# Second-layer scales by a logarithm and an exponential on ScalarE instead of powers of two

## The chip, the core and the metric

One Trainium2 chip, one of its cores. The metric is the time of one execution on the device, in microseconds (us); lower is better. The kernel before takes 1286.33 us, the median of three runs (1284.23 to 1288.01). A difference of about 0.3%, some 3.9 us, is what a measurement of this kernel can tell from no change.

The engines are called as the profile calls them: PE (matrix multiply; PEld are its weight loads), DVE (VectorE), ACT (ScalarE), POOL (GpSimd) and SP (SyncE, here only a queue that issues DMA transfers). Each engine runs its own list of instructions strictly in the order in which they were recorded; an instruction that waits for a semaphore holds up everything behind it on that engine.

## What is computed

Eight batches of eight heads, 576 rows, 64 columns per head. The attention keeps only scores within `tau` of the row's maximum; a two-layer network with a rational function between the layers follows.

```python
scores = matmul(q, k.T) / sqrt(64)
scores = where(scores >= max(scores) - tau, scores, -1e9)
attn = exp(scores - max(scores)); attn /= sum(attn) + 1e-9
x = attn @ v                                  # 4608 x 512 after the heads are put side by side
h = x @ w_in                                  # 512 x 2048
P = a[0] + a[1]*h + a[2]*h**2 + a[3]*h**3
Q = 1 + abs(b[0])*abs(h) + abs(b[1])*h**2
out = (P / (Q + 1e-6)) @ w_out                # 2048 x 512
```

## The kernel before, in words

**Attention.** The work is cut into units: one pair of heads and one block of 128 rows (64 for the last, odd block). A unit is: scores on PE (L840 to L851), the negated row maximum on DVE (L857, or L859 for an odd block), a thresholding Prelu and an Exp with row sums on ACT (L872, L876), the reciprocal of the sums (L881 or L883 for the sum's scaling on ACT or DVE, L887 for the reciprocal), the probabilities split into two 16-bit parts (L894 on ACT or DVE through the helper `times`, L898 on DVE), a transpose by DMA from SP (L908), and the product with the values on PE (L969). The first batch transposes on PE instead (L914, L921, L926) and uses L952.

**Network.** A step (`moe_ops`) takes 256 rows of `x` and up to four blocks of 128 hidden columns: first layer on PE (L1092), its result scaled out by ACT (L1101), then about ten element-wise passes on DVE and ACT (L1103 to L1144: `f_A`, `f_r2`, `f_q`, `f_r3`, `f_ln`, `f_inv`, `f_e`, `f_n`, `f_g`, `f_gh`, `f_gl`), then the second layer on PE (L1153) and its evacuation (`f_o`, L1159 or L1164). There are 73 steps.

**Scales.** The second layer is fed with 16-bit pieces, so its left operand is brought into range by a scale per batch. `scale_of` (L1275) makes it for each batch and each set of weight groups: 12 runs in all, ten named `gs_m` and two named `gs_r`. A run is: a bound of the result by four short instructions on POOL (`f_bound`), six short DVE instructions on one to four columns (`f_scales`: minimum, mask to an even power of two, maximum, a root made by integer arithmetic on the exponent, two products), and one logarithm on ACT (`f_ln_r`). `f_inv` (L1123) takes its logarithm, `f_n` (L1133) the product `m2r`, and `f_o` the factor `down`.

**Weights.** Both weight matrices arrive as 64-bit words and are decoded and scaled in 32 pieces during the first part (`decode_ops`, `group_ops`: L528 to L610); loads go out from POOL (L573).

**The order.** Every instruction is recorded as an `op` with a key and estimated durations for the engines that could run it; `Plan.order` places the ops one after another by keys, readiness, buffers and prices per engine, and so decides both the order on each engine and, for some ops (`FLEX` and `can`: for example the 16-bit copy `f_gh`, or L881/L883), which of ACT and DVE runs it. `START`, `EARLY` and `PRICE` weigh an engine's time up to about 70 us, up to `EARLY_END`, and after it; `LEAD`, `SPACING`, `ENDK` and `ENDS` set the keys of the network's steps, `WHEN` and `AHEAD_RANK` those of the weights, `V0` and `V1` those of the value loads. In planned idle time of PE before 400 us the plan puts filler matmuls on the identity matrix (L1383), which compute nothing that is used.

Of the kernel before, what the change touches and what calls it, by code (L numbers as in the profile page):

```python
# [31 lines left out]
ENDK, ENDS = 4.7452, 10.130284218  # L32

WHEN = [(-4.7413, 1.827956817), (5.5534, 0.8332), (13.0267, 0.2709), (15.0744, 0.5122)]

V0, V1 = -4.003497408, -3.629280468

SINGLE = 21

# [23 lines left out]

MASK, EVEN = 0x7F800000, 0x7F000000

BOUND = {"POOL": 1.8}

STEEP = 2.0 ** 100

ALL = 2.0 ** 100  # L70
# [3 lines left out]
UP = 2.0 ** -14  # L74
TPD = 1.3

AHEAD_RANK = 2.703269966

AHEAD = 3

# [48 lines left out]
class Plan:  # L129
# [158 lines left out]
def masked_attention_rational_ffn(  # L288
# [16 lines left out]
    P = 128  # L305
# [748 lines left out]
    def moe_ops(ck, f0, nb, p, begins, ends, soon, gs):  # L1054
# [174 lines left out]
        if ends:  # L1229
            prev = None  # L1230
            obox = {}
            through = f0 + nb == NF
            part = Hold("t", 2)
            for tt in range(2):
                old = sums.get((ck, tt))
                obox[tt] = {}
                if old is None:
                    ho = obox[tt]["hold"] = Hold("u", 1) if through else part
                    o = op("ACT", 0.477, p + 0.2 * nb + 1.8, lambda tt=tt, old=old: f_o(tt, old), [last_g2[tt], prev], [ho] if through or tt == 0 else [], [ah[tt]])
                else:  # L1240
                    ho = old[1]
                    o = op("DVE", 0.663, p + 0.2 * nb + 1.8, lambda tt=tt, old=old: f_o(tt, old), [last_g2[tt], prev, old[2]], (), [ah[tt]])
# [11 lines left out]
    def consts(gs):  # L1254


        if gs not in consts_of:
            n = len(gs)
            tab = const.tile([P, n + 3], F32, name=f"gc_{gs[0]}_{n}")
            m2, wmax, top, dn = tab[:, 0:n], tab[:, n:n + 1], tab[:, n + 1:n + 2], tab[:, n + 2:n + 3]  # L1260

            def f_consts():
                io = so[:, gs[0]:gs[-1] + 1]
                nc.vector.tensor_reduce(wmax, wn[:, gs[0]:gs[-1] + 1], AX.X, ALU.max)
                nc.vector.tensor_reduce(top, io, AX.X, ALU.max)
                nc.vector.tensor_scalar(dn, top, osc, 2.0 ** -13, ALU.mult, ALU.mult)
# [3 lines left out]
                nc.vector.tensor_scalar(m2, m2, -2.0 ** 65, None, ALU.mult)  # L1270
            o = op("DVE", 0.95, w_key(gs[-1], 2 * NC), f_consts, [co_b] + [z[y] for z in (wn_done, so_done) for y in gs])
            consts_of[gs] = o, m2, wmax, dn
        return consts_of[gs]

    def scale_of(ck, gs):  # L1275


        kind, b, _ = ck
        run = kind, b, gs
        if run not in scales_of:  # L1280
            n = len(gs)
            done, m2, wmax, dn = consts(gs)
            tab = const.tile([P, 2 * n + 4], F32, name=f"gs_{kind}{b}_{gs[0]}_{n}")
            m2r, lnr = tab[:, 0:n], tab[:, n:2 * n]
            H, s, R, down = (tab[:, 2 * n + i:2 * n + i + 1] for i in range(4))

            def f_top():
                nc.vector.tensor_reduce(R, isx[:, 4 * b:4 * b + 4], AX.X, ALU.max)

            def f_bound():  # L1290
                x = isx[:, b:b + 1] if kind == "m" else R
                e = engines[plan.eng]
                e.tensor_scalar(H, x, wmax, 1.0, ALU.mult, ALU.mult)
                e.tensor_scalar(s, H, c2, H, ALU.add, ALU.mult)
                e.tensor_scalar(s, s, c1, H, ALU.add, ALU.mult)
                e.tensor_scalar(s, s, c0, ct, ALU.add, ALU.mult)

            def f_scales():
                nc.vector.scalar_tensor_tensor(s, H, c1s, s, ALU.add, ALU.min)
                nc.vector.tensor_single_scalar(s.bitcast(I32), s.bitcast(I32), EVEN, ALU.bitwise_and)  # L1300
                nc.vector.tensor_scalar(s, s, SMALL, None, ALU.max)
                nc.vector.tensor_scalar(R.bitcast(I32), s.bitcast(I32), -0.5, float(197 << 23), ALU.mult, ALU.add)
                nc.vector.tensor_scalar(m2r, m2, R, None, ALU.mult)
                nc.vector.tensor_scalar(down, s, dn, None, ALU.mult)
# [6 lines left out]
            o = [done] + [isx_done[x] for x in bs]  # L1311
# [114 lines left out]
```

## Time and profile before

| | before |
|---|---|
| median of 3 runs | 1286.33 us |
| the profiled execution | 1288.7 us |
| its span on the core | 1286.9 us |
| mean granted PE clock | 0.981 |
| PE busy | 1225.7 us (95%) |
| DVE busy | 1224.1 us (95%) |
| ACT busy | 1114.2 us (87%) |
| POOL busy | 262.4 us (20%) |

The span lies 1.8 us inside the profiled execution's own time, and that execution took 2.4 us more than the median of the three. In the views below a group's row gives the busy time of all its instructions, the mean of one in ns, and behind the second bar the idle time of the engine just ahead of them with what ended it. In a timeline a row's first number is the start, the second the duration, both in us; neighbouring short instructions overlap a little, so the step from one start to the next is what an instruction costs its engine. Matmul ends are modelled.

### The profile page before, as it was taken

The page shows a single profiled execution, that of the slowest core. Times are in us where ns is not written, and L with a number is a line of the kernel's source. Part 1 is how long each engine was busy: PE and PEld are TensorE (multiplying, and loading weights), DVE is VectorE, ACT ScalarE, POOL GpSimd, SP SyncE. Part 2 cuts the span into 40 slices and gives each one's busy share as a digit, 9 for nine tenths or more (in the row PEclk, how much of TensorE's full clock was granted, in tenths as well). Part 3 has the DMA queues.
Part 4 walks back from the last instruction along what each step waited for, and adds up shares of the span by engine and source line. Part 5 has one row for each costly group of instructions (what it writes and reads, how often), then busy time and mean ns, then how long its engine had stood idle before and what let it go on. Part 6 is the DMA issues. An engine that isn't in the chain of part 4 may idle for free.

```text
span 1286.9 us, 25594 instructions
## 1 busy us (share of the span) xinstructions
PE 1225.7 (95%) x9520; PEld 799.3 (62%) x9520; DVE 1224.1 (95%) x1871; ACT 1114.2 (87%) x2183; POOL 262.4 (20%) x528
## 2 busy tenths in 40 slices
PE   7899899999999989899999799999999989999998
PEld 6566676566666656566666466656666655656674
DVE  5798999999999999999999899999999999999897
ACT  5898999899997988899999799999899998986564
POOL 3112010013412242134211241134212331000000
PEclk8899999999999999999999899999999989999999
DMA  9434325468545765577645666576756756643001
GB/s 251 152 116 122 111 65 113 94 131 156 123 110 104 142 130 112 113 139 149 122 101 100 119 137 129 95 148 122 149 88 129 140 95 115 123 94 68 17 1 33
DMA packets 338380, 146.67 MB, mean 114 GB/s; under 512 B 314416, under 2 KB 320720, under 8 KB 338256
## 3 DMA queue, kind: packets, MB, share of 16 engines
q1 hardware_dynamic: 316816, 88.19, 38.4%
q0 software_dynamic: 21120, 56.25, 15.8%
q8 instruction: 75, 1.23, 0.4%
q10 hardware_dynamic: 320, 0.59, 0.2%
q14 instruction: 49, 0.40, 0.1%
HBM read 60.30 MB, written 9.44 MB: 54 GB/s over the span
## 4 chain that ended last, share of the span: by engine, by line
PE 29%; DVE 22%; issue 6%; ACT 5%; POOL 1%; DMA 1%; DVEq 0%; ACTq 0%; POOLq 0%
PE banks L1153 12%; PE banks L1092 11%; DVE e L898 5%; PE banks L969 3%; DVE st L857 3%; PE banks L851 3%; DVE g L1144 2%; DVE t L1126 1%; DVE t L1129 1%; DVE t L1112 1%; DVE t L1115 1%; DVE t L1133 1%; DVE t L1136 1%; ACT e L872 1%; DVE hi L339 1%
## 5 line engine op out<-in xcount | busy, mean ns | idle before, releaser
L1153 PE MATMUL banks<-wo,g 128*128 128x512 f16 x1728 | 401.7, 381 | 8.0 <-DVE g L1144 8.0
L1092 PEld LDWEIGHTS <-wi 128*128 128x128 f16 x3456 | 335.2, 99 | 109.6 <-issue 57.8
L1092 PE MATMUL banks<-x,wi 128*128 128x256 f16 x3072 | 362.3, 275 | 19.3 <-ACT t L1101 16.7
L1153 PEld LDWEIGHTS <-g 128*128 128x128 f16 x1728 | 162.5, 99 | 226.7 <-issue 40.9
L876 ACT ACTIVATE e<-e,cf 128x576 f32<-128x576 f32 x288 | 221.3, 775 | 0.3
L872 ACT ACTIVATE e<-banks,st 128x576 f32<-128x576 f32 x288 | 208.6, 736 | 12.6 <-DVE st L866 9.9
L898 DVE SCALAR_TENSOR_TENSOR e<-e,st,hi 128x576 f16<-128x576 f32 x252 | 203.6, 808 | 4.5 <-ACT hi L337 4.2
L337 ACT ACTIVATE hi<-e,st 128x576 f16<-128x576 f32 x183 | 139.0, 768 | 49.5 <-DVE st L887 38.4
L857 DVE TENSOR_REDUCE st<-banks 128x2 f32<-128x1152 f32 x128 | 171.9, 1343 | 10.4 <-PE banks L851 9.9
L851 PE MATMUL banks<-KK,QQ 64*128 64x512 f32 x512 | 148.5, 658 | 0.0
L969 PEld LDWEIGHTS <-V 128*64 128x64 f16 x2520 | 104.2, 111 | 30.6 <-issue 28.1
L969 PE MATMUL banks<-pT,V 128*64 128x256 f16 (+1 forms) x2520 | 121.7, 250 | 1.5 <-DMA pT<-e 1.5
L1101 ACT ACTIVATE t<-banks,hsc 128x512 f32<-128x512 f32 (+1 forms) x192 | 106.4, 573 | 18.1 <-PE banks L1092 17.7
L1119 ACT ACTIVATE t<-t,co 128x1024 f32<-128x1024 f32 (+1 forms) x73 | 82.6, 1132 | 21.5 <-DVE t L1126 20.4
L1112 DVE SCALAR_TENSOR_TENSOR t<-t,co 128x1024 f32<-128x1024 f32 (+1 forms) x73 | 91.9, 1260 | 0.5 <-ACT t L1101 0.5
L1115 DVE SCALAR_TENSOR_TENSOR t<-t,co 128x1024 f32<-128x1024 f32 (+1 forms) x73 | 91.9, 1259 | 0.0
L680 POOL DMA_DIRECT2D QQ<-in_qT_dram x42 | 22.2, 529 | 341.5 <-PE banks L840 192.6
L1144 DVE TENSOR_TENSOR g<-t,g 128x1024 f16<-128x1024 f32 (+1 forms) x73 | 87.6, 1200 | 0.1
L1126 DVE SCALAR_TENSOR_TENSOR t<-t,co,t 128x1024 f32<-128x1024 f32 (+1 forms) x65 | 81.7, 1257 | 0.0
L1129 DVE SCALAR_TENSOR_TENSOR t<-t,co,t 128x1024 f32<-128x1024 f32 (+1 forms) x62 | 77.9, 1257 | 1.9 <-ACT t L1123 1.9
L1136 DVE SCALAR_TENSOR_TENSOR t<-t,co,t 128x1024 f32<-128x1024 f32 (+1 forms) x63 | 79.2, 1257 | 0.1
L724 POOL DMA_DIRECT2D V<-in_v_dram x24 | 18.8, 785 | 272.0 <-PE banks L969 169.8
(186 smaller groups left out, 1690.7 us busy)
## 6 DMA issues: line engine op xcount, KB each, us to landing
KK<-in_kT_dram POOLq DMA_DIRECT2D x84, 144.0 KB, 3.5
t<-in_w_in_dram POOLq DMA_DIRECT2D x16, 512.0 KB, 5.6
t<-in_w_out_dram POOLq DMA_DIRECT2D x16, 512.0 KB, 5.0
V<-in_v_dram POOLq DMA_DIRECT2D x24, 256.0 KB, 4.4
QQ<-in_qT_dram POOLq DMA_DIRECT2D x42, 144.0 KB, 3.2
out_dram<-u POOLq DMA_DIRECT2D x22, 256.0 KB, 3.4
QQ<-in_qT_dram POOLq DMA_DIRECT2D x42, 128.0 KB, 3.4
KK<-in_kT_dram SPq DMA_DIRECT2D x24, 144.0 KB, 3.2
```

The lines of the kernel that those rows point to most:

```text
L337: nc.scalar.activation(dst, src, AF.Identity, scale=factor)
L851: nc.tensor.matmul(d, QQ[r, t * P:(t + 1) * P], KK[r, REM:S], **one)
L857: nc.vector.tensor_reduce(box["st"][:, 0:2], box["both"], AX.X, ALU.max, negate=True)
L872: nc.scalar.activation(ev(hh), box["s"][hh], AF.Prelu, scale=SCALE, bias=box["st"][:, 2 + hh:3 + hh], alpha=STEEP)
L876: nc.scalar.activation(e, e, AF.Exp, scale=passes, accum_out=box["st"][:, 4 + hh:5 + hh])
L898: nc.vector.scalar_tensor_tensor(box["lo"][:, c], ev(hh), box["st"][:, 6 + hh:7 + hh], box["hi"][:, c], ALU.mult, ALU.subtract)
L969: nc.tensor.matmul(dst, V[:, c * P + head * D:c * P + (head + 1) * D], rhs, start=c == 0 and n == 0, stop=c == NT and n == 2)
L1092: nc.tensor.matmul(d, wi_tile(c, f0 + j, hl), x[:, c, :], start=c == 0 and n == 0, stop=c == NC - 1 and n == 2)
L1101: nc.scalar.activation(box["h3"][:, 2 * k:2 * k + 2, sl], psv[:, :, sl], AF.Identity, scale=hsc[:, b2, (f0 + 2 * k) // NC:(f0 + 2 * k) // ...
L1112: nc.vector.scalar_tensor_tensor(box["r"], box["h"], a2, box["h"], ALU.add, ALU.mult)
L1144: nc.vector.tensor_tensor(box["g", x][:, 1, 0:w], box["r"][:, j0 * CT:j1 * CT], box["g", x][:, 0, 0:w], ALU.subtract)
L1153: nc.tensor.matmul(acc[tt], box["g", x][:, y, o:o + P], wo[:, x, f % NC, z], start=begins and j == n == 0, stop=ends and j == nb - 1 and n ...
```

## The change

The six DVE instructions of `f_scales` become two: the minimum stays (`f_min`), and a reciprocal is added (`f_one`). What lay between is done on ACT, as five short activations (`f_roots`): the logarithm `l` of the bound, its exponential with factor -1/2 (the scale `R`, now any number and not a power of two), `l` halved, the product of the group constants with `R`, and their logarithm plus `l`. The logarithm of the group constants alone (`ln2`) is made once per set of groups. Two more short instructions go to POOL: the square of `R` (`f_square`) and, after the reciprocal on DVE, the factor `down` (`f_down`). `f_inv` now waits for `f_roots` only; `f_o` waits for `f_down` as well (`scaled`). The bound on POOL is no longer an op with a table of engines, but is on POOL as it was.

Beside this the planner's numbers are changed, among them these:

```diff
-LEAD, SPACE0, SPACING = 4.776489494, 2.7365, 2.235134465
+LEAD, SPACE0, SPACING = 5.974676841, 2.7365, 2.235134465
-START = {"ACT": 2.072266916, "DVE": 3.23844158}
+START = {"ACT": 2.072266916, "DVE": 2.724283317}
```

`ENDS` goes from 10.13 to 8.45, `AHEAD_RANK` from 2.70 to 1.91, `PRICE` of DVE from 2.95 to 2.54, `EARLY_END` from 1185.1 to 1164.8, `V1` from -3.63 to -3.35, `ENDK` from 4.75 to 5.49, and the third pair of `WHEN` from 13.03 to 13.58.

```diff
-            def f_scales():
+            def f_min():
                 nc.vector.scalar_tensor_tensor(s, H, c1s, s, ALU.add, ALU.min)
-                nc.vector.tensor_single_scalar(s.bitcast(I32), s.bitcast(I32), EVEN, ALU.bitwise_and)
-                nc.vector.tensor_scalar(s, s, SMALL, None, ALU.max)
-                nc.vector.tensor_scalar(R.bitcast(I32), s.bitcast(I32), -0.5, float(197 << 23), ALU.mult, ALU.add)
-                nc.vector.tensor_scalar(m2r, m2, R, None, ALU.mult)
-                nc.vector.tensor_scalar(down, s, dn, None, ALU.mult)
-
-            def f_ln_r():
-                nc.scalar.activation(lnr, m2r, AF.Ln, scale=-0.5)
+
+            def f_roots():
+                nc.scalar.activation(l, s, AF.Ln, bias=small_)
+                nc.scalar.activation(R, l, AF.Exp, scale=-0.5)
+                nc.scalar.activation(l, l, AF.Identity, scale=-0.5)
+                nc.scalar.activation(m2r, m2, AF.Identity, scale=R)
+                nc.scalar.activation(lnr, ln2, AF.Identity, bias=l)
+
+            def f_square():
+                nc.gpsimd.tensor_tensor(s, R, R, ALU.mult)
+
+            def f_one():
+                nc.vector.reciprocal(s, s)
+
+            def f_down():
+                nc.gpsimd.tensor_scalar(down, s, dn, 1.0, ALU.mult, ALU.mult)
...
-            o = op(BOUND, 0, p, f_bound, o)
-            o = op("DVE", 0.8, p, f_scales, [o])
-            o = op("ACT", 0.25, p, f_ln_r, [o])
+            o = op("POOL", 1.8, p, f_bound, o)
+            o = op("DVE", 0.15, p, f_min, [o])
+            o = o1 = op("ACT", 1.1, p, f_roots, [o])
+            o = op("POOL", 0.4, p, f_square, [o])
+            o = op("DVE", 0.1, p, f_one, [o])
+            o = [o1, op("POOL", 0.4, p, f_down, [o])]
```

The instructions that are left stand in another order, since all of them were placed anew. Three places follow, in the order in which the engine runs its rows; a name with a number is one buffer, and the changed kernel numbers lines and buffers a little differently.

DVE before, in batch 0, between the first maximum over the weight pieces (L449 on `wm`) and the one over the values (L449 on `vm`). L737 reduces the fourth pair's values `V`, which a DMA brings; L331 evacuates a transposed block; L344 decodes a weight piece.

```order
L449 TENSOR_REDUCE sc_86<-wm 128x1
L455 TENSOR_SCALAR u_68<-ident,sc_86 128x128
L331 COPY pT_76<-banks 128x128
L737 TENSOR_REDUCE vm_218<-V_140 128x1
L344 ISA t_97<-t_97,u_70 128x512x2
L887 RECIPROCAL st_80<-st_80 128x2
L449 TENSOR_REDUCE sc_87<-vm_218 128x1
```

DVE in the changed kernel, the rows that end with the same reduction of the fourth pair's values (line 342 here is 344 before, 329 is 331, 337 is 339).

```order
L472 TENSOR_SCALAR sw<-sc_86 128x1
L474 RECIPROCAL sw<-sw 128x1
L914 TENSOR_SCALAR u_70<-ident,st_80 128x128
L337 TENSOR_SCALAR wi<-t_95,sw 128x512 x2
L610 SCALAR_TENSOR_TENSOR wi<-t_95,sw,wi 128x512 x2
L610 SCALAR_TENSOR_TENSOR wi<-t_96,sw,wi 128x512 x2
L329 COPY pT_77<-banks 128x128
L342 ISA t_97<-t_97,u_69 128x512x2
L887 RECIPROCAL st_81<-st_81 128x2
L583 TENSOR_REDUCE wm<-t_97 128x1
L737 TENSOR_REDUCE vm_220<-V_142 128x1
```

The reduction that waits for the fourth pair's values stood two places behind the weights' maximum; now the whole scaling of the first weight group (L465 to L474) and its splitting (L337, L610) go ahead of it, with a score reduction, 21 instructions in all.

DVE in the changed kernel, around one of the twelve scale runs, from the minimum (L1304 there) to the reciprocal (L1317 there); L784 splits the next batch's values, L1129 is a pass of the network. Before, the six instructions of `f_scales` stood together.

```order
L1304 SCALAR_TENSOR_TENSOR gs_m_0_4_161<-gs_m_0_4_161,co 128x1
L784 SCALAR_TENSOR_TENSOR V_141<-V_141,sx,u_68 128x640
L784 SCALAR_TENSOR_TENSOR V_142<-V_142,sx,u_69 128x640
L329 COPY V_141<-u_68 128x640
L329 COPY V_142<-u_69 128x640
L1129 SCALAR_TENSOR_TENSOR t_95<-t_95,co,t_96 128x1024
L1317 RECIPROCAL gs_m_0_4_161<-gs_m_0_4_161 128x1
```

Five other instructions now stand between the two; while they run, ACT's roots and POOL's square have to be done.

More of the change, by code (lines that the diff above doesn't have):

```diff
@@ L28 @@
 B2, B3, BA, B1, BH = [(0, 1, 2), (3, 4, 5)], [(0, 1, 2)], [(3,), (4,), (5,)], [(7,), (6,), (5,)], [(5,), (6,)]
-LEAD, SPACE0, SPACING = 4.776489494, 2.7365, 2.235134465
-ENDK, ENDS = 4.7452, 10.130284218
-WHEN = [(-4.7413, 1.827956817), (5.5534, 0.8332), (13.0267, 0.2709), (15.0744, 0.5122)]
-V0, V1 = -4.003497408, -3.629280468
+LEAD, SPACE0, SPACING = 5.974676841, 2.7365, 2.235134465
+ENDK, ENDS = 5.488906476, 8.452439532
+WHEN = [(-4.7413, 1.827956817), (5.5534, 0.8332), (13.580547557, 0.2709), (15.0744, 0.5122)]
+V0, V1 = -4.003497408, -3.352127285
 SINGLE = 21
@@ L64 @@
 MASK, EVEN = 0x7F800000, 0x7F000000
-BOUND = {"POOL": 1.8}
 STEEP = 2.0 ** 100
@@ L75 @@
 TPD = 1.3
-AHEAD_RANK = 2.703269966
+AHEAD_RANK = 1.912895801
 AHEAD = 3
@@ L88 @@
          "vc": {"ACT": 0.7, "DVE": 0.25}, "twice": {"ACT": 0.2, "DVE": 0.13}}
-START = {"ACT": 2.072266916, "DVE": 3.23844158}
+START = {"ACT": 2.072266916, "DVE": 2.724283317}
 START_END = 70.459703715
 EARLY = {"ACT": 2.0183, "DVE": 2.9268}
-EARLY_END = 1185.086141893
-PRICE = {"ACT": 0.7389, "DVE": 2.949233976}
+EARLY_END = 1164.835153503
+PRICE = {"ACT": 0.7389, "DVE": 2.538788989}
 TOL = {"PE": 0.098890645, "ACT": 0.1137, "DVE": 0.0398, "POOL": 0.1, "DMA": 0, "GD": 0}
@@ L375, in masked_attention_rational_ffn @@
     ones = bass.AP(one.tensor, one.offset, [list(one.ap[0]), [0, P]])
+    small_ = const.tile([P, 1], F32, name="small")
+    nc.vector.memset(small_, SMALL)
     one16 = const.tile([P, 2], BF16, name="one16")
@@ L1204, in moe_ops @@
         ln = op("ACT", act(nb) + 0.09, p + 0.7, f_ln, [q, r3])
+        sd, scaled = sd
         iv = [op("ACT", act(x[2] - x[1]) + 0.09, p + 0.75, lambda x=x: f_inv(*x), [ln, sd]) for x in parts]
@@ L1238, in moe_ops @@
                     ho = obox[tt]["hold"] = Hold("u", 1) if through else part
-                    o = op("ACT", 0.477, p + 0.2 * nb + 1.8, lambda tt=tt, old=old: f_o(tt, old), [last_g2[tt], prev], [ho] if through or tt == 0 else [], [ah[tt]])
+                    o = op("ACT", 0.477, p + 0.2 * nb + 1.8, lambda tt=tt, old=old: f_o(tt, old), [last_g2[tt], prev, scaled], [ho] if through or tt == 0 else [], [ah[tt]])
                 else:
                     ho = old[1]
-                    o = op("DVE", 0.663, p + 0.2 * nb + 1.8, lambda tt=tt, old=old: f_o(tt, old), [last_g2[tt], prev, old[2]], (), [ah[tt]])
+                    o = op("DVE", 0.663, p + 0.2 * nb + 1.8, lambda tt=tt, old=old: f_o(tt, old), [last_g2[tt], prev, scaled, old[2]], (), [ah[tt]])
                 prev = o
@@ L1258, in consts @@
             n = len(gs)
-            tab = const.tile([P, n + 3], F32, name=f"gc_{gs[0]}_{n}")
-            m2, wmax, top, dn = tab[:, 0:n], tab[:, n:n + 1], tab[:, n + 1:n + 2], tab[:, n + 2:n + 3]
+            tab = const.tile([P, 2 * n + 3], F32, name=f"gc_{gs[0]}_{n}")
+            m2, ln2 = tab[:, 0:n], tab[:, n:2 * n]
+            wmax, top, dn = (tab[:, 2 * n + i:2 * n + i + 1] for i in range(3))
             def f_consts():
@@ L1269, in f_consts, with f_ln2 @@
                 nc.vector.tensor_scalar(m2.bitcast(I32), m2.bitcast(I32), 1, MASK, ALU.logical_shift_right, ALU.bitwise_and)
-                nc.vector.tensor_scalar(m2, m2, -2.0 ** 65, None, ALU.mult)
-            o = op("DVE", 0.95, w_key(gs[-1], 2 * NC), f_consts, [co_b] + [z[y] for z in (wn_done, so_done) for y in gs])
-            consts_of[gs] = o, m2, wmax, dn
+                nc.vector.tensor_scalar(m2, m2, -2.0 ** 72, None, ALU.mult)
+            def f_ln2():
+                nc.scalar.activation(ln2, m2, AF.Ln, scale=-0.5)
+            key = w_key(gs[-1], 2 * NC)
+            o = op("DVE", 1.2, key, f_consts, [co_b] + [z[y] for z in (wn_done, so_done) for y in gs])
+            consts_of[gs] = [o, op("ACT", 0.25, key, f_ln2, [o])], m2, ln2, wmax, dn
         return consts_of[gs]
@@ L1281, in scale_of @@
             n = len(gs)
-            done, m2, wmax, dn = consts(gs)
-            tab = const.tile([P, 2 * n + 4], F32, name=f"gs_{kind}{b}_{gs[0]}_{n}")
+            done, m2, ln2, wmax, dn = consts(gs)
+            tab = const.tile([P, 2 * n + 5], F32, name=f"gs_{kind}{b}_{gs[0]}_{n}")
             m2r, lnr = tab[:, 0:n], tab[:, n:2 * n]
-            H, s, R, down = (tab[:, 2 * n + i:2 * n + i + 1] for i in range(4))
+            H, s, R, l, down = (tab[:, 2 * n + i:2 * n + i + 1] for i in range(5))
             def f_top():
@@ L1291, in f_bound @@
                 x = isx[:, b:b + 1] if kind == "m" else R
[L1292 to L1296, printed above, removed]
-            def f_scales():
[L1299 to L1304, printed above, removed]
-            def f_ln_r():
-                nc.scalar.activation(lnr, m2r, AF.Ln, scale=-0.5)
+                nc.gpsimd.tensor_scalar(H, x, wmax, 1.0, ALU.mult, ALU.mult)
+                nc.gpsimd.tensor_scalar(s, H, c2, H, ALU.add, ALU.mult)
+                nc.gpsimd.tensor_scalar(s, s, c1, H, ALU.add, ALU.mult)
+                nc.gpsimd.tensor_scalar(s, s, c0, ct, ALU.add, ALU.mult)
+            def f_min():
+                nc.vector.scalar_tensor_tensor(s, H, c1s, s, ALU.add, ALU.min)
+            def f_roots():
[10 more added lines that the diff above has]
+                nc.gpsimd.tensor_scalar(down, s, dn, 1.0, ALU.mult, ALU.mult)
             bs = [b] if kind == "m" else range(4 * b, 4 * b + 4)
@@ L1310, in scale_of @@
             rank, plan.rank = plan.rank, p
-            o = [done] + [isx_done[x] for x in bs]
+            o = done + [isx_done[x] for x in bs]
             if kind == "r":
                 o = [op("DVE", 0.08, p, f_top, o)]
-            o = op(BOUND, 0, p, f_bound, o)
-            o = op("DVE", 0.8, p, f_scales, [o])
-            o = op("ACT", 0.25, p, f_ln_r, [o])
+            o = op("POOL", 1.8, p, f_bound, o)
[4 more added lines that the diff above has]
+            o = [o1, op("POOL", 0.4, p, f_down, [o])]
             plan.rank = rank
```

2 lines of the change are left out of this document (1 added, 1 removed).

## The prediction

> **What bounds the kernel now.** First the page: the busy time of each engine, then the span in 40 slices, each digit the busy tenths.
>
> ```profile
> PE 1225.7 (95%) x9520; PEld 799.3 (62%) x9520; DVE 1224.1 (95%) x1871; ACT 1114.2 (87%) x2183; POOL 262.4 (20%) x528
> ...
> PE   7899899999999989899999799999999989999998
> ...
> DVE  5798999999999999999999899999999999999897
> ```
>
> PE and DVE are both full for nearly the whole span; ACT has an eighth to spare. An average over stages hides where each is the limit, so next the busy times by stretch (start and end, length, then PE, PEld, DVE, ACT, POOL, and the granted clock).
>
> ```profile
> 0.00:32.20 32.20, 25.07 (x129) 19.85 (x130) 17.27 (x55) 17.95 (x37) 10.31 (x37) 0.84 0.93 251
> 32.20:64.30 32.10, 27.24 (x158) 16.90 (x157) 24.80 (x64) 27.12 (x63) 4.40 (x12) 0.89 0.48 152
> ...
> 200.00:300.00 100.00, 98.26 (x802) 65.89 (x801) 100.00 (x136) 91.90 (x169) 8.33 (x17) 1.00 0.61 121
> ...
> 700.00:800.00 100.00, 91.18 (x743) 56.93 (x741) 93.51 (x137) 89.51 (x176) 29.78 (x59) 0.97 0.64 123
> ...
> 1200.00:1220.00 20.00, 20.00 (x139) 13.33 (x138) 14.11 (x13) 9.16 (x18) 0.00 (x0) 1.00 0.08 27
> ```
>
> Three stages. **Start**: of the first 64.3 us DVE works 42.1 and is idle 22.2, a third of all its idle time (1286.9 - 1224.1 = 62.8). **Middle**: DVE is the limit, 100 of 100 us, with rare holes such as 6.5 us in 700 to 800. **End**: PE is full, DVE is not. The chain that ended last says the same of the end (start, length, what):
>
> ```profile
> 1168.48 11.90 PE banks L1092 x108
> ...
> 1182.14 10.46 PE banks L1153 x48
> ...
> 1267.51 15.55 PE banks L1153 x72
> ```
>
> From 1168 us it is one run of matmuls. A matmul of the first layer costs 11.90/108 = 0.110 us, one of the second 15.55/72 = 0.216 us.
>
> **The DVE instructions taken out.** One scale run in the timeline, engine DVE:
>
> ```profile
> 764.44 0.22 DVE L1299 SCALAR_TENSOR_TENSOR gs_m<-gs_m,co 128x1 f32<-128x1 f32 x1
> 764.69 0.15 DVE L1300 TENSOR_SCALAR gs_m<-gs_m 128x1 int32<-128x1 int32 x1
> 764.88 0.15 DVE L1301 TENSOR_SCALAR gs_m<-gs_m 128x1 f32<-128x1 f32 x1
> 765.07 0.15 DVE L1302 TENSOR_SCALAR gs_m<-gs_m 128x1 int32<-128x1 int32 x1
> 765.26 0.23 DVE L1303 TENSOR_SCALAR gs_m<-gc,gs_m 128x4 f32<-128x4 f32 x1
> 765.40 0.21 DVE L1304 TENSOR_SCALAR gs_m<-gs_m,gc 128x1 f32<-128x1 f32 x1
> 765.52 0.81 DVE L898 SCALAR_TENSOR_TENSOR e<-e,st,hi 128x576 f16<-128x576 f32 x1
> ```
>
> L1300 to L1304 go: 765.52 - 764.69 = 0.83 us a run, 12 runs, **-10.0 us**. The reciprocal that comes in is a short instruction like L1300, 0.15 us, 12 times: +1.8 us. The net is -8.2 us of DVE.
>
> **What DVE gets instead.** The plan spends this. Counting both orders, DVE takes over seven of the 16-bit copies `f_gh` (24 become 31), sixteen scalings of the row sums (37 become 53), four weight scalings (6 become 10), and in ones and twos six thresholds, two `hi`, two value copies, three block copies and a few more, while it gives up three value scalings and six `x` copies. The rows with the largest terms, and ACT's rows for the same work:
>
> ```profile
> L331 DVE CAST g<-t 128x1024 f16<-128x1024 f32 (+1 forms) x24 | 16.2, 674 | 0.3
> L883 DVE TENSOR_SCALAR st<-st 128x2 f32<-128x2 f32 (+1 forms) x37 | 5.8, 157 | 1.1 <-ACT e L876 1.1
> L339 DVE TENSOR_SCALAR wi<-t,sw 128x512 f16<-128x512 f32 x6 | 2.7, 479 | 0.0
> L329 ACT CAST g<-t 128x1024 f16<-128x1024 f32 (+1 forms) x49 | 50.5, 1031 | 11.8 <-DVE t L1136 11.8
> L881 ACT ACTIVATE st<-st 128x2 f32<-128x2 f32 (+1 forms) x123 | 24.7, 201 | 1.2
> L864 ACT ACTIVATE st<-st,cf 128x2 f32<-128x2 f32 (+1 forms) x119 | 34.2, 287 | 12.4 <-DVE st L857 10.4 <-DVE st L859 1.5
> ```
>
> 7 x 0.674 + 16 x 0.157 + 4 x 0.479 = 9.1 us by durations. Instructions that don't depend on each other overlap by some 0.07 us (L1303 above is 0.23 long and the next starts 0.14 later), so 27 of them cost about 1.9 less: 7.2. The ones and twos come to +1 (an estimate from their groups' means). DVE's own work is therefore **unchanged**: -8.2 + 8.2, within 2 us either way. The saving does not reach the end by itself.
>
> ACT loses 7 x 1.03 + 16 x 0.20 + 6 x 0.29 = 12.1 us and some 4 us of smaller things, and gains five short activations a run for one: two like L881 (0.20), three with an operand per row like L864 (0.29), 1.27 - 0.20 = 1.07 us, 12 times +12.8. It stays near 1111 us, the slackest of the three.
>
> **Where time can go: the start.** DVE's waits in the first 130 us, by what it waited for, and the stretch that holds the longest:
>
> ```profile
> DVE vm L737 <- DMA V<-in_v_dram: 8.9, 4, 4.0
> ```
>
> ```profile
> 33.08 0.29 DVE L331 COPY pT<-banks 128x128 f32<-128x128 f32 x1 [1.65 <-PE banks L926]
> 37.41 0.82 DVE L737 TENSOR_REDUCE vm<-V 128x1 f32<-128x640 f32 x1 [4.05 <-DMA V<-in_v_dram]
> ```
>
> The fourth pair's values land at 37.4 us and DVE stands still for them for 4.05 us, with a 1.65 us wait just ahead. In the new order 21 instructions stand between the weights' maximum and that reduction, about 7 us of work by their rows' kinds. SP's loads up to this one are in the same order, so the values land no later, and DVE should reach L737 near 40 us, after them. The block copy ahead of it now belongs to a block that PE has finished earlier. I count **-4.05 and -1.65 us**. The bounds: 0, if the weights' maximum or the score reduction put ahead is itself late, and -8.9 if all four waits for values vanished; the other three keep their places. I take -5.7 because these two rows are the ones whose neighbours changed.
>
> Adding the steps from one start to the next (each kind's median) over all DVE rows ahead of the last of the 128 double reductions L857 gives 1115.0 us of work before and 1118.4 in the new order: **+3.4 us** ahead of it, given back behind it.
>
> **The end.** Behind the last attention-value matmul PE had 354 matmuls of the first layer and 288 of the second; now 348 and 282: 6 x 0.110 + 6 x 0.216 = **-1.95 us**, at the place where PE alone is the limit. The fillers on PE fall from 132 to 99 (the profile records each as two):
>
> ```profile
> L1383 PE MATMUL banks<-ident 128*128 128x128 f32 x264 | 39.4, 301 | 1.4 <-POOL ident masks.py:199 1.4
> ```
>
> 39.4/132 = 0.30 us each. They lie in the start, where the plan saw PE idle, so I count the 33 at nothing; if PE is wanted there they are worth up to 9.9 us.
>
> **The new handoff.** Before, POOL handed over to DVE once a run; now also from ACT to POOL and back to DVE for the reciprocal. Here is what such a handoff can do (first scale run, all engines):
>
> ```profile
> 112.16 1.28 DVE L1112 SCALAR_TENSOR_TENSOR t<-t,co 128x1024 f32<-128x1024 f32 x1
> ...
> 112.29 2.48 POOL L1294 TENSOR_SCALAR gs_m<-gs_m,co 128x1 f32<-128x1 f32 x1
> ...
> 114.87 0.34 POOL L1295 TENSOR_SCALAR gs_m<-gs_m,co 128x1 f32<-128x1 f32 x1
> ...
> 115.68 0.22 DVE L1299 SCALAR_TENSOR_TENSOR gs_m<-gs_m,co 128x1 f32<-128x1 f32 x1 [1.05 <-POOL gs_m L1296]
> ```
>
> A POOL step takes 0.34 us alone, but 2.48 while DVE runs its long passes, and DVE then waited 1.05. The groups of L1299, with the waits behind the second bar, and two passes that can be in the way:
>
> ```profile
> L1299 DVE SCALAR_TENSOR_TENSOR gs_m<-gs_m,co 128x1 f32<-128x1 f32 x10 | 2.1, 211 | 1.3 <-POOL gs_m L1296 1.0
> ...
> L1299 DVE SCALAR_TENSOR_TENSOR gs_r<-gs_r,co 128x1 f32<-128x1 f32 x2 | 0.4, 219 | 2.3 <-POOL gs_r L1296 2.3
> ...
> L784 DVE SCALAR_TENSOR_TENSOR V<-V,sx,u 128x640 f16<-128x640 f32 x28 | 23.7, 877 | 0.0
> ...
> L1119 ACT ACTIVATE t<-t,co 128x1024 f32<-128x1024 f32 (+1 forms) x73 | 82.6, 1132 | 21.5 <-DVE t L1126 20.4 <-DVE t L1115 0.9
> ```
>
> All twelve waits before add up to 3.6 us, 1.0 and 2.3 of it in three runs. In the new order 2.4 to 4.8 us of DVE work stand between minimum and reciprocal; the way round needs about 1.1 us if nothing is in the way (two activations 0.5, one square 0.34, three handoffs). So I count the new wait at 0, like that of the nine `gs_m` runs that hardly waited; uncovered it costs 1.05 a run, 12.6 us. Behind a waiting reciprocal stand the network's passes, and PE waits for those. POOL's key and query loads queue behind the square; POOL is 20% busy, so I count their delay at nothing too.
>
> The Trainium skill bears on this place ("SBUF — State Buffer", section "Who interferes with whom"): a VectorE instruction with two SBUF inputs and a GpSimd instruction that reads SBUF exclude each other for the whole instruction. The 2.48 us agree with it, since L1112 and L1115 are such. By that rule the two L784 between minimum and reciprocal would hold up the square, which speaks against the change; the sum by it is that of the second rival below, the sum without it is the one that follows.
>
> **The sum**, against the profiled execution: 1288.7 + 3.4 (DVE ahead of the last scores) - 5.7 (start) - 1.95 (end) + 0 (handoff) = 1284.5. That execution was 2.4 us above the median of 1286.33, so **1282** for the median of the changed kernel, 0.3% less. The forecast's own range is 1278 to 1286.
>
> **Rivals.**
> *The gain of the start is lost again*: another wait takes the place of the 4.05 us, for weights or for a score block. For it: DMA was 0.93 busy in the first stretch. Against it: in 32 to 64 us it is 0.48. Then 1288.7 + 3.4 - 1.95 - 2.4 = 1287.7 if all 5.7 are lost, 1284.9 with half.
>
> *The handoff is uncovered* (the slower side): ACT may be inside a 1.13 us pass when the minimum is ready, and the square may be held for two L784 (0.88 us each): 1.1 + 1.1 + 1.8 = 4.0 against covers of mostly 2.9, so about 1.1 us a run: 1282 + 13 = 1295. From 0.7 us a run on the kernel is slower by over 0.3%. Against it: those nine `gs_m` runs.
>
> *The middle's hole closes too*:
>
> ```profile
> 714.06 8.65 DMA pT<-hi
> ...
> 723.60 0.82 DVE L898 SCALAR_TENSOR_TENSOR e<-e,st,hi 128x576 f16<-128x576 f32 x1 [3.97 <-ACT hi L337]
> ...
> 732.32 1.36 DVE L857 TENSOR_REDUCE st<-banks 128x2 f32<-128x1152 f32 x1 [1.99 <-PE banks L851]
> ```
>
> A transpose landed after 8.65 us behind a burst on POOL's queue (loads, two stores, two value loads), and DVE lost 3.97 + 1.99. Gone, the time is 1276. Against it: POOL's order keeps exactly this burst. *That the change doesn't do what it says* is half true already: DVE's short instructions go, but its work does not.
>
> **How the numbers follow.** Forecast 0.50, on both sides of the bound of 1282.5, about what a measurement can tell from no change (0.31 faster, 0.19 the same); start lost 0.19 (same); handoff uncovered 0.18 (slower); hole closed 0.13 (faster). Faster 0.44, same 0.38, slower 0.18. The range 1272 to 1295 takes in the hole and most of the handoff.
>
> **What would show it.** DVE busy 1222 to 1227 us; no wait of 4 us before 40 us at the value reduction; waits at the reciprocal under 3 us in all; 348 and 282 matmuls behind the last L969 and a chain of PE there; `f_gh` on DVE 31 times. I am wrong if the reciprocal's waits add up to over 8 us, if DVE's idle time in the first 64 us stays at 22, or if a hole like that at 714 us shows up more than once.

## The result, and the profile after

The changed kernel takes 1293.2 us, the median of four runs (1292.27 to 1293.93), beside 1286.8 us for the kernel before on the same chip: a ratio of 1.0052, with a 95% interval of 1.0035 to 1.0069. It is slower by 0.5%, where the prediction had 0.3% faster. Repeated on two other chips it came out nearer: 1288.84 us (1.0019, 1.0007 to 1.0030) and 1290.64 us (1.0026, 1.0015 to 1.0037), so the loss is 2 to 6.4 us. The profiled execution took 1293.93 us, 5.2 us more than the profiled one of before.

The page of the changed kernel, its busy times and the 40 slices of PE and DVE:

```profile
PE 1221.4 (95%) x9454; PEld 790.5 (61%) x9454; DVE 1223.7 (95%) x1855; ACT 1108.3 (86%) x2203; POOL 283.6 (22%) x552
...
PE   7898899999999998999999999999899979999998
...
DVE  5899999999999999999999999999899989999897
```

DVE does the same amount of work as before (1224.1 us), as forecast. What differs is where it stands still: the digit for the second slice rose, and two 8s appeared late in the middle. The busy times by stretch show it (changed kernel; start, end and length, then PE, PEld, DVE):

```profile
0.00:64.30 64.30, 51.75 (x308) 37.37 (x308) 45.42 (x131) 47.67 (x103) 14.54 (x48) 0.89 0.69 201
64.30:200.00 135.70, 122.42 (x905) 83.46 (x903) 130.25 (x326) 124.32 (x278) 26.29 (x55) 0.97 0.36 107
200.00:700.00 500.00, 484.58 (x3832) 311.23 (x3829) 490.73 (x675) 454.12 (x902) 124.30 (x227) 0.98 0.63 122
700.00:800.00 100.00, 93.86 (x781) 59.66 (x779) 96.72 (x134) 85.31 (x179) 32.11 (x61) 0.98 0.62 123
...
900.00:1000.00 100.00, 93.29 (x696) 59.24 (x694) 94.24 (x120) 84.01 (x162) 22.33 (x44) 0.97 0.60 115
1000.00:1100.00 100.00, 92.37 (x795) 59.55 (x792) 93.10 (x144) 88.88 (x183) 31.95 (x57) 0.98 0.61 117
```

The same view of the kernel before, for the stretches that the prediction did not show:

```profile
64.30:200.00 135.70, 126.21 (x947) 89.49 (x946) 127.51 (x327) 125.75 (x278) 20.75 (x47) 0.99 0.35 103
200.00:700.00 500.00, 485.74 (x3894) 314.75 (x3893) 495.37 (x690) 455.05 (x893) 115.65 (x219) 0.99 0.63 123
...
900.00:1000.00 100.00, 96.44 (x781) 63.67 (x779) 98.82 (x127) 91.26 (x176) 21.69 (x43) 0.98 0.63 124
1000.00:1100.00 100.00, 93.53 (x763) 59.70 (x762) 96.98 (x150) 89.02 (x174) 26.97 (x50) 0.97 0.60 113
```

Length less DVE's busy time is its idle time:

| stretch, us | idle before | idle after | difference |
|---|---|---|---|
| 0 to 64.3 | 22.2 | 18.9 | -3.3 |
| 64.3 to 200 | 8.2 | 5.4 | -2.8 |
| 200 to 700 | 4.6 | 9.3 | +4.7 |
| 700 to 800 | 6.5 | 3.3 | -3.2 |
| 900 to 1000 | 1.2 | 5.8 | +4.6 |
| 1000 to 1100 | 3.0 | 6.9 | +3.9 |

The start gained 6.1 us and the old hole at 714 to 732 us half closed, and the middle lost 13.2 us. Two new holes make most of that. The first is at the new reciprocal. DVE's groups of the minimum (L1304 in this kernel) and of the reciprocal (L1317), waits behind the second bar:

```profile
L1304 DVE SCALAR_TENSOR_TENSOR gs_m<-gs_m,co 128x1 f32<-128x1 f32 x10 | 2.1, 211 | 0.8 <-POOL gs_m L1301 0.6
L1317 DVE RECIPROCAL gs_m<-gs_m 128x1 f32<-128x1 f32 x10 | 1.6, 157 | 5.2 <-POOL gs_m L1314 5.1
L1304 DVE SCALAR_TENSOR_TENSOR gs_r<-gs_r,co 128x1 f32<-128x1 f32 x2 | 0.4, 220 | 3.5 <-POOL gs_r L1301 3.5
...
L1317 DVE RECIPROCAL gs_r<-gs_r 128x1 f32<-128x1 f32 x2 | 0.3, 156 | 0.6 <-POOL gs_r L1314 0.6
```

10.1 us of waits where before had 3.6, and 4.47 of them in one place. The timeline there, all engines (start, length, engine, line; the idle time ahead of the row in brackets):

```profile
1047.88 0.20 DVE L1304 SCALAR_TENSOR_TENSOR gs_m<-gs_m,co 128x1 f32<-128x1 f32 x1
...
1048.79 0.27 POOL L1298 TENSOR_SCALAR gs_r<-gs_r,gc 128x1 f32<-128x1 f32 x1
...
1049.05 0.20 ACT L1308 ACTIVATE gs_m<-gs_m 128x1 f32<-128x1 f32 x1
...
1051.14 0.34 POOL L1301 TENSOR_SCALAR gs_r<-gs_r,co 128x1 f32<-128x1 f32 x1
...
1054.27 0.55 POOL L687 DMA_DIRECT2D KK<-in_kT_dram  x1 [2.79 <-issue]
...
1055.35 1.03 POOL L691 DMA_DIRECT2D KK<-in_kT_dram  x2
...
1056.40 0.20 POOL L1314 TENSOR_TENSOR gs_m<-gs_m 128x1 f32<-128x1 f32 x1
1056.63 0.16 DVE L1317 RECIPROCAL gs_m<-gs_m 128x1 f32<-128x1 f32 x1 [4.47 <-POOL gs_m L1314]
...
1061.93 0.78 ACT L335 ACTIVATE hi<-e,st 128x576 f16<-128x576 f32 x1 [4.16 <-DVE st L887]
```

The root is ready at 1049.25 us, and the square that needs it takes 0.20 us, yet runs at 1056.40. In between POOL works through what was recorded ahead of the square: the bound of another run (to 1051.48), then four key loads, the first of which itself stood for 2.79 us. The square is behind POOL's loads and another run's bound, not ahead of them. Behind the reciprocal, DVE's L887 is late and ACT loses 4.16 us.

The second new hole is at 905 us, on POOL and ACT:

```profile
891.88 0.68 ACT L1164 ACTIVATE u<-banks,gs_m 128x512 f32<-128x512 f32 x1
...
893.76 2.67 POOL L1300 TENSOR_SCALAR gs_m<-gs_m,co 128x1 f32<-128x1 f32 x1
...
899.63 0.56 POOL L1173 DMA_DIRECT2D out_dram<-u  x1
...
902.41 0.20 POOL L1314 TENSOR_TENSOR gs_m<-gs_m 128x1 f32<-128x1 f32 x1
...
907.51 0.69 ACT L1164 ACTIVATE u<-banks,gs_m 128x512 f32<-128x512 f32 x1 [4.62 <-DMA out_dram<-u]
...
908.32 0.17 DVE L887 RECIPROCAL st<-st 128x2 f32<-128x2 f32 x1 [3.06 <-ACT st L881]
```

ACT has written `u` by 892.56 us; its store is issued 7.1 us later, behind a bound and five loads, and the next write of that buffer waits for it. The store also lands late, 7.9 us after its issue, where the median of the stores that POOL issues from `u` is 3.4 us in the same profile. ACT came to the next write at 902.9 us, 3.3 us after the issue, so with the median landing, or with an earlier issue, there would hardly have been a wait (an estimate from these figures). Before, no wait of ACT at this line ended with a store.

### The profile page after: what moved, and what is told of

The parts are those of the page before. It is cut to its first block, busy times and chain, and to the rows that moved or that the text cites. A ratio compares the mean times of both kernels' runs of the same rounds, so it can differ in the third digit from the quotient of the medians.

```text
span 1291.8 us, 25493 instructions
## 1 busy us (share of the span) xinstructions
PE 1221.4 (95%) x9454; PEld 790.5 (61%) x9454; DVE 1223.7 (95%) x1855; ACT 1108.3 (86%) x2203; POOL 283.6 (22%) x552
## 4 chain that ended last, share of the span: by engine, by line
PE 46%; DVE 34%; issue 8%; ACT 6%; DMA 3%; POOL 2%; SPq 0%; DVEq 0%; ACTq 0%; POOLq 0%
PE banks L1153 18%; PE banks L1092 14%; DVE e L898 6%; PE banks L851 5%; PE banks L969 5%; DVE st L857 4%; DVE t L1136 2%; DVE g L1144 2%; DVE t L1115 2%; DVE t L1126 2%; DVE t L1129 2%; DVE t L1133 2%; DVE t L1112 2%; PE banks L840 1%; ACT e L872 1%
## 5 line engine op out<-in xcount | busy, mean ns | idle before, releaser
L857 DVE TENSOR_REDUCE st<-banks 128x2 f32<-128x1152 f32 x128 | 172.0, 1344 | 13.9 <-PE banks L851 13.3
L969 PEld LDWEIGHTS <-V 128*64 128x64 f16 x2520 | 106.2, 112 | 33.2 <-issue 30.9
L969 PE MATMUL banks<-pT,V 128*64 128x256 f16 (+1 forms) x2520 | 123.2, 252 | 1.4 <-DMA pT<-e 1.2
L1126 DVE SCALAR_TENSOR_TENSOR t<-t,co,t 128x1024 f32<-128x1024 f32 (+1 forms) x68 | 85.6, 1259 | 0.0
L1129 DVE SCALAR_TENSOR_TENSOR t<-t,co,t 128x1024 f32<-128x1024 f32 (+1 forms) x58 | 72.9, 1257 | 3.2 <-ACT t L1123 3.2
L1136 DVE SCALAR_TENSOR_TENSOR t<-t,co,t 128x1024 f32<-128x1024 f32 (+1 forms) x60 | 75.4, 1257 | 0.1
```

Source lines behind the costliest of these rows:

```text
L857: nc.vector.tensor_reduce(box["st"][:, 0:2], box["both"], AX.X, ALU.max, negate=True)
L969: nc.tensor.matmul(dst, V[:, c * P + head * D:c * P + (head + 1) * D], rhs, start=c == 0 and n == 0, stop=c == NT and n == 2)
```

## The experiments

Three theories. *POOL's queue* (the expectations call it 'way round POOL'): the way from ACT over POOL back to DVE is long because the square is recorded behind POOL's transfers. *Order*: the planner's new numbers bring collisions in the middle whatever the scales are made of. *Port*: POOL's steps are held by DVE's passes with two inputs from SBUF, the prediction's own rival. All ratios are against the kernel before on the same chip.

### The scale chain and the numbers, each alone

The new chain with the old numbers, and the old chain with the new ones:

```diff
-LEAD, SPACE0, SPACING = 5.974676841, 2.7365, 2.235134465
+LEAD, SPACE0, SPACING = 4.776489494, 2.7365, 2.235134465
...
```

> The new scale chain (logarithm, exponential, square, reciprocal) with the planner's numbers of before (LEAD, ENDK, ENDS, WHEN, V1, AHEAD_RANK, START, EARLY_END, PRICE). Theory 'way round POOL': the reciprocal still waits for the square, together with L1304's waits more than 6 us in all, and the time stays at 1289 us or above. Theory 'order' (the new numbers bring the middle's collisions, whatever the chain): the time goes to 1287 us or below, because 8 us of VectorE's short instructions are gone and the old order is back.

> The old scale chain (five short VectorE instructions per run, no square or reciprocal) with the planner's numbers of the change. Theory 'way round POOL': the 6 us of waits go, VectorE gets back its 8 us of short instructions unless the plan moves work off it, so 1285 to 1290 us, and the gap of 4 us near 1056 us is not there. Theory 'order': as slow as the change or slower, 1292 to 1300 us, with gaps in the stages 400-600 and 900-1100 us as after the change.

Measured: the new chain with old numbers 1303.03 us (1.0128, 1.0105 to 1.0150), the old chain with new numbers 1293.59 us (1.0040, 1.0026 to 1.0053). The first keeps 6.1 us of waits at the reciprocal, but loses more at the end: the last run of matmuls in its chain of waits takes 27.84 us where before had 15.55, and DVE waits 14.0 us for ACT's L1123, most of it there:

```profile
1268.99 27.84 PE banks L1153 x119
```

```profile
DVE t L1129 <- ACT t L1123: 14.0, 7, 3.1
```

The second has no reciprocal to wait for and is as slow as the change, with 3.5 us more DVE work (1227.2); but the holes near 905 and 1056 us are not in it (DVE idle 3.4 and 0.7 us in 900 to 1000 and 1000 to 1100 us). The first lies in the range of *POOL's queue* and far outside that of *Order*, the second the other way about, without the gaps that *Order* named. Chain and numbers each lose when put into the other's kernel, so the loss can't be divided between them in this way. The next runs keep the planned order and change one thing in it.

### The square away from POOL's transfers

First the square on DVE, just ahead of the reciprocal; then POOL's loads and stores recorded behind the square of their run (from 430 us of the plan on: seven runs, in five places).

```diff
             def f_square():
-                nc.gpsimd.tensor_tensor(s, R, R, ALU.mult)
+                pass
             def f_one():
+                nc.vector.tensor_tensor(s, R, R, ALU.mult)
                 nc.vector.reciprocal(s, s)
```

```diff
+        open_ += mark == "bound"
+        if open_ and o.eng == "GD":
+            held.append(o)
+            continue
```

> The change with the same planned order, but the square is computed on VectorE just ahead of the reciprocal instead of on POOL. Theory 'way round POOL': the 5.7 us of waits at the reciprocal go, 14 runs or so of one more short instruction cost about 2 us, so 1289 to 1291 us. Theory 'order': nothing is won, 1293 to 1296 us. Theory 'port' (POOL's steps are held by VectorE's passes): as the first theory.

> The change with the same planned order, but from 430 us on the loads and stores that POOL issues between a bound and its square are issued behind that square. Theory 'way round POOL', by the queue of DMA issues: the reciprocal's waits fall from 5.7 us to below 1 us and the time to 1287 to 1290 us, less what the later loads cost. Theory 'port': the waits at the reciprocal stay at 4 us or more, for POOL's square would be held whatever it is queued behind. Theory 'order': 1292 to 1295 us whatever the waits at the reciprocal do.

Measured: square on DVE 1285.95 us (0.9987, 0.9978 to 0.9997); transfers behind the squares 1284.9 us (0.9977, 0.9965 to 0.9988). Both are below before, and 2 to 3 us below the ranges of *POOL's queue*, which had been reckoned from the 1293.2 us of another chip. In the second POOL still makes the square beside the same DVE passes, and the reciprocal hardly waits:

```profile
L1317 DVE RECIPROCAL gs_m<-gs_m 128x1 f32<-128x1 f32 x10 | 1.5, 154 | 0.2 <-POOL gs_m L1314 0.2
```

So *Port* falls as the cause, and *Order* as the only one. Next the change with neither square nor reciprocal, POOL's queue otherwise untouched, and then with the loads behind as well:

```diff
-                nc.gpsimd.tensor_scalar(down, s, dn, 1.0, ALU.mult, ALU.mult)
+                nc.scalar.activation(s, l, AF.Exp, scale=-2.0)
+                nc.scalar.activation(down, s, AF.Identity, scale=dn)
```

> The change with the same planned order and POOL's queue as it was, without the square and the reciprocal: the scale comes back from the logarithm by a second exponential, and ScalarE makes both it and the scale down in POOL's place. 24 more short ScalarE instructions (0.2 to 0.3 us each, 6 us of an engine that is 86% busy), no POOL square, no VectorE reciprocal (-1.9 us). Theory 'the square queued behind POOL's DMA issues': as the run with the square on VectorE (1286 us) less its 1.8 us of squares and 1.9 us of reciprocals, so 1282 to 1286 us. If ScalarE's share counts: 1287 to 1292 us.

> Both together: neither square nor reciprocal, ScalarE makes both scales, and POOL's loads and stores behind the bounds of their run as well. If the way round POOL is the whole loss and ScalarE has room, it is the fastest of all: 1281 to 1284 us. If ScalarE's 24 more instructions cost as much as they take (6 us), 1288 to 1291 us.

Measured: 1287.45 us (0.9998, 0.9987 to 1.0010) and 1284.3 us (0.9973, 0.9960 to 0.9986). The first is 1.5 us above its range; its hole at 905 us is still there, and so are 4.5 us of waits at the minimum for the bound, which is behind loads too. By the time alone it lies in the range of the other case, that ACT's 24 more instructions cost what they take. The second has the same instructions and is 4 us below that case's 1288 to 1291, so they are not the main cost. It is no faster than moving the loads alone (0.3 us above its range).

### Which place

> As the run with POOL's loads and stores behind the squares (1284.9 us), but only at the last two runs (planned after 980 us; key and query loads near 1050 us). The page of the change shows 4.5 us of wait at the reciprocal there and 1.0 us at the lower bound. If the direct waits are what counts, -5 to -6 us from the change's 1293.2: 1287 to 1288.5 us. If what follows them on ScalarE and TensorE counts as well: below 1286 us, and the other sites are worth under 1 us.

> As the run with POOL's loads and stores behind the squares, but only at the sites planned between 430 and 980 us; the last two runs stay as in the change. Direct waits there in the change: 2.5 us at the lower bound near 465 us, 0.4 to 0.7 us at reciprocals. Expected 1290 to 1292 us, with the wait of 4 to 5 us near 1056 us still there. The two parts together should add to the 8.3 us that all sites brought.

Measured: the last place alone 1284.09 us (0.9963, 0.9948 to 0.9977), the others alone 1288.63 us (1.0009, 0.9997 to 1.0021). The others came out 1.4 us below the range expected of them, with the wait near 1056 us still there. The last place carries the whole gain of the five; the others don't add to it. Its gain of 9.1 us against the change's 1293.2 is too much for 5.6 us of waits, but these runs were on another chip than the change's.

### The second hole, and a planner that knows of one queue

`Plan.order` keeps two free times, `GD` for POOL's transfers and `POOL` for its arithmetic, as if they ran side by side. One kernel moves the store ahead of the bound near 895 us, on top of the last place's edit; one makes the planner use a single time:

```diff
+        if 865.0 < o.start < 870.0 and o.eng in ("POOL", "GD"):
+            if getattr(o, "mark", "") != "store":
+                behind.append(o)
+                continue
```

```diff
             free[e] = end = t + o.dur
+            if e in ("POOL", "GD"):
+                free["POOL"] = free["GD"] = end
```

> The change itself once more, beside the two edits of this batch, on one chip. The run with only the last site's loads behind the squares stood 9.1 us below the change's 1293.2 us, more than the 5.6 us that the waits at that site lost. If the runs differ between chips by 1 to 3 us, the change comes out at 1289.5 to 1292 us here; if the rest is a true effect of the edit, at 1292 to 1294 us again, with waits of 4.5 us near 1056 us in either case.

> As the run with the last site's loads behind the squares (1284.1 us), and near 895 us POOL issues the store of u ahead of the bound and the two loads, at about 890 us instead of 897 us. Theory 'POOL's queue makes the second gap too': ScalarE's wait of 4.1 us for u's store at L1164 goes, VectorE's gaps of 2.5 and 1.7 us behind it (905 and 914 us) shrink, and the time falls by 2 to 4 us to 1280 to 1282 us; the bound starts 0.6 us later, which costs nothing. Rival (the store lands late whenever it is issued, because the transposing DMAs fill the queues): the wait at L1164 stays over 3 us and the time at 1283 to 1285 us.

> The change, with the planner told that POOL's loads and stores and its arithmetic share one queue (it plans them as two, side by side). This re-plans everything behind 150 us, so the other numbers no longer fit the plan they were chosen for. Theory 'way round POOL': the waits at the reciprocal fall from 5.8 to under 2 us; theory 'the rest of the order decides': the time is nonetheless above 1290 us, by other gaps; below 1286 us if the queue was all that the plan had wrong.

Measured on one chip: the change 1288.84 us (1.0019), both edits 1278.05 us (0.9936, 0.9922 to 0.9950), one queue in the planner 1302.49 us (1.0126, 1.0108 to 1.0144). The change is 0.7 us below the range for chips that differ, and both edits are 2 us below theirs. The change's waits near 905 and 1056 us are the same in the repeat, so it is the chip or the execution that moves the total by a few us. The planner with one queue does what it should at the reciprocal and loses elsewhere (this kernel's lines are two higher):

```profile
L1319 DVE RECIPROCAL gs_m<-gs_m 128x1 f32<-128x1 f32 x10 | 1.6, 158 | 1.2 <-POOL gs_m L1316 1.1
L1306 DVE SCALAR_TENSOR_TENSOR gs_r<-gs_r,co 128x1 f32<-128x1 f32 x2 | 0.4, 218 | 4.9 <-POOL gs_r L1303 4.9
```

That order is new from the first part on; where it loses was not followed further.

### Four corners on one chip

Neither edit, the last place's loads, the store, both:

> The change as it is, the corner 'neither' of four kernels on one chip. It gave 1293.2 us beside 1286.8 of before on one chip (+6.4) and 1288.8 beside 1286.8 on another (+2.0). Expected again between 2 and 6 us over before, with the waits of 4.5 us near 1056 us and of 3 to 5 us near 905 us whatever the time.

> The corner 'last site only': POOL's key and query loads behind the last two squares. The waits that it takes away are 5.6 us of VectorE; if they are worth their length, 4.5 to 7 us under the change on the same chip; if the 9.1 us of the first comparison were the edit's, 8 to 10 us.

> The corner 'store only': the store of u near 895 us ahead of the bound and the loads, the last site as in the change. If the gaps of 5.5 us behind ScalarE's wait for the store are worth their length, 5 to 7 us under the change on the same chip, that is at before's time or up to 4 us under it. If it works only together with the other edit (9.1 and 6 us were measured one on the other): under 3 us.

> The corner 'both' (1278.1 us on another chip, 8.8 us under before). If the two edits add: the sum of the other two corners' gains within 2 us, some 10 to 13 us under the change, 1277 to 1280 us.

| | median, us | against the change | ratio to before (1287.67 us) |
|---|---|---|---|
| the change | 1290.64 | | 1.0026 (1.0015 to 1.0037) |
| last place's loads behind the squares | 1284.50 | -6.1 | 0.9982 (0.9968 to 0.9997) |
| store ahead of the bound | 1286.30 | -4.3 | 0.9989 (0.9978 to 0.9999) |
| both | 1278.82 | -11.8 | 0.9932 (0.9920 to 0.9943) |

6.1 + 4.3 = 10.4, so the edits add within the 2 us expected; the store alone is 0.7 us short of its range. The places in the profiles: with the loads moved the square runs 3.1 us after the minimum, and the reciprocal no longer waits:

```profile
1043.01 0.20 DVE L1304 SCALAR_TENSOR_TENSOR gs_m<-gs_m,co 128x1 f32<-128x1 f32 x1
...
1046.13 0.20 POOL L1314 TENSOR_TENSOR gs_m<-gs_m 128x1 f32<-128x1 f32 x1
...
1046.77 0.15 DVE L1317 RECIPROCAL gs_m<-gs_m 128x1 f32<-128x1 f32 x1
...
1049.16 0.59 POOL L680 DMA_DIRECT2D QQ<-in_qT_dram  x1
```

With the store moved (that kernel's profile) it is issued at 889.60 us, 0.3 us after its data, and ACT's next write waits for nothing. It landed 2.7 us after its issue, so it doesn't land late whenever it is issued. The edit takes away the late issue and the slow landing together, and does not tell them apart:

```profile
888.62 0.68 ACT L1164 ACTIVATE u<-banks,gs_m 128x512 f32<-128x512 f32 x1
889.60 0.67 POOL L1173 DMA_DIRECT2D out_dram<-u  x1 [8.42 <-DVE st L883]
...
899.53 0.67 ACT L1164 ACTIVATE u<-banks,gs_m 128x512 f32<-128x512 f32 x1
```

With both, the two stretches, in the same view as above:

```profile
900.00:1000.00 100.00, 96.67 (x753) 62.81 (x753) 99.48 (x125) 89.07 (x169) 19.89 (x39) 1.00 0.59 111
1000.00:1100.00 100.00, 96.72 (x847) 62.38 (x845) 98.73 (x152) 94.47 (x195) 31.80 (x57) 1.00 0.67 122
```

DVE's 5.8 and 6.9 us of idle time are 0.5 and 1.3 there. With both edits the kernel is faster than the change and than before: 8.9 us under before on this chip, 8.8 on the other.

## Why the prediction was wrong, step by step

*DVE's own work unchanged* (-8.2 + 8.2): right. 1223.7 us, inside 1222 to 1227. The copies and the scalings went over as counted:

```profile
L329 DVE CAST g<-t 128x1024 f16<-128x1024 f32 (+1 forms) x31 | 21.0, 676 | 0.1
...
L883 DVE TENSOR_SCALAR st<-st 128x2 f32<-128x2 f32 (+1 forms) x53 | 8.7, 164 | 1.7 <-ACT e L876 1.7
```

*+3.4 us ahead of the last L857*: right in size. That row starts at 1168.5 us instead of 1160.9, 7.6 later, and 4.7 of these are more idle time ahead of it; 2.9 are work.

*The start, -5.7 us*: half right in the mechanism, and near in the sum by luck. DVE's idle time to 64.3 us fell by 3.3 us, that to 200 us by 6.1. The waits for values fell from 8.9 to 4.5 us, none of 4 us is left, and the two waits counted (4.05 and 1.65 us) are gone, but a score reduction now put ahead took up some of it:

```profile
DVE vm L737 <- DMA V<-in_v_dram: 4.5, 2, 3.4
```

```profile
35.67 1.36 DVE L857 TENSOR_REDUCE st<-banks 128x2 f32<-128x1152 f32 x1 [2.93 <-PE banks L851]
```

The other 2.8 us came between 64 and 200 us, where no term had put them.

*The end, -1.95 us*: right. 348 and 282 matmuls stand behind the last L969, and from there to the end of the span it is 102.8 us instead of 104.8.

*The handoff at 0*: the step that failed. The prediction said that POOL's key and query loads queue behind the square. It set the way round (1.1 us without obstacles) against the DVE work between minimum and reciprocal, and took POOL's load of 20% for the chance that something is in the way. The waits at the reciprocal came to 5.8 us, above the 3 that were to show the forecast right and below the 8 that were to show it wrong. Near 1056 us the cover was 4.3 us (1047.88 to 1052.16), as forecast, and the way round 8.5, because another run's bound and the loads stood ahead of the square. With the loads behind the squares the time is 6.1 us shorter: that is the size of the term counted at 0. In the planned order POOL's rows can be read too, and there the loads stand between a bound and its square; the prediction showed only DVE's rows of this place. The busy share was the wrong measure for a second reason: it leaves out the time for which a transfer stands at the head of the queue with everything else behind it. The first query load and the first value load of a pair in the changed kernel (idle time of POOL ahead of them behind the second bar):

```profile
L680 POOL DMA_DIRECT2D QQ<-in_qT_dram x42 | 22.3, 532 | 282.6 <-PE banks L840 149.4 <-PE banks L851 125.9 <-issue 7.1
...
L724 POOL DMA_DIRECT2D V<-in_v_dram x24 | 19.4, 808 | 262.5 <-PE banks L969 237.8 <-PE banks L952 21.3 <-issue 3.3
```

That is 545 us of 1291.8 that the 22% does not hold. Transfers stand between bound and square in nine of the twelve runs; the other eight of the nine waited only 1.1 us in all at the reciprocal, since their cover was long enough, or nearly.

The rival *handoff uncovered* had the right sign with the wrong mechanism: a small loss in each run, by ACT's pass and the port. The loss was mostly one run's, 4.47 of the 5.8 us. On the port, the row L1300 of the changed kernel takes 2.67 us at 893.76 us, beside two DVE passes L784, and 0.33 us at its shortest. That agrees with the rule that the prediction takes from the Trainium skill ("SBUF — State Buffer", section "Who interferes with whom"). But the square took 0.20 us at 902.41 and at 1056.40 us, and the wait went when only the queue was changed. On the queue, the Trainium skill ("DMA: Bandwidth & Descriptors", section "SWDGE vs HWDGE vs iDMA") says that GpSimd itself computes the descriptors of a transfer issued from it; the trace agrees, 0.52 to 0.57 us of POOL for each of these loads.

*The middle's hole*: taken to stay, with a chance of 0.13 to close. The stretch from 700 to 800 us went from 6.5 to 3.3 us of idle time, so that rival came half true. The change without any edit left 2.0 and 3.2 us there in its two repeats and both edits left 1.8, so the rest of the hole differs between executions and is not what the edits closed.

*A hole like that at 714 us more than once* was named as a sign of error, and the one at 905 us is it. No term had it. It is not part of the handoff: it goes with the store alone (-4.3 us).

Put together from the runs: -4.2 forecast, some 3 more from the old hole, +6.1 at the last place, +4.3 at the store: about +3, between the +2.0 and +6.4 measured. With both collisions taken away the planned order gains 8.9 us, as much as the forecast's 4.2 and the 4.7 of the old hole (6.5 to 1.8) together. These sums mix forecast terms with measured ones and leave out the idle time between 200 and 700 us, so that they come out so well is in part luck. What stays open: those 4.7 us more of idle time between 200 and 700 us, in waits of 2.5 us and less, that neither edit touched; and why the other eleven runs of the change's first repeat lay 5 to 8 us under its profiled 1295.3 us, though both waits stand in all three profiles of it (its clock was 0.980, the median of the others 0.984; by the line fitted in the last section, an estimate, some 3 us go with that).

## What to carry to other kernels

Where an engine issues transfers and computes, read its row order at each place where another engine will wait for its arithmetic: a busy share of 20% says nothing about the 7 us of bound, standing load and issues ahead of a 0.2 us step. A planner that gives such an engine two free times can make handoffs over it look short and stores look early. Two edits of POOL's order were worth more (11.8 us) than the whole change was forecast to bring; planning all anew with one free time was not the cure (1302.49 us). When a change re-plans an order, count what the new order brings into each burst on the transfer queues, not only what it takes out of the waits you know.

## What the runs showed of the hardware that was not expected

A transfer at the head of POOL's queue can stand with nothing in the profile that releases it ("issue"), and what is recorded behind it stands too: 2.79 us at the key load near 1054 us, 7.07 us at a query load at 770.26 us. With the loads moved the same key load stood 1.14 us, and nobody waited.

The time goes with the granted TensorE clock even where DVE is the limit: the kernel before, 29 times on one chip, went from 1283.0 us at a clock of 0.985 to 1292.2 us at 0.981, and a straight line through the 29 gives 0.77 us for each 0.001. From 0.980 to 0.987, the clocks that occurred there, that is 5 us or 0.4%. These 29 don't tell which of the two causes the other. The four corners show that a hole lowers the clock of its stretch:

| clock granted in | 900 to 1000 us | 1000 to 1100 us |
|---|---|---|
| the change | 0.97 | 0.97 |
| last place's loads behind the squares | 0.98 | 1.00 |
| store ahead of the bound | 1.00 | 0.97 |
| both | 1.00 | 1.00 |

Each edit brings back the clock of the stretch whose hole it closes, so part of a lower mean clock is a trace of the holes.
